# A new order of the engine pieces, and block 1 normalized with ScalarE's negated mean

## The chip, the cores and the metric

The kernel runs on one core of one Trainium2 chip. The core has a matrix engine (TensorE, "PE" in the profile, with its weight loads shown apart as "PEld"), VectorE ("DVE"), ScalarE ("ACT"), GpSimd ("POOL"), SyncE ("SP", here only a queue that issues DMAs) and sixteen DMA engines. Each engine works through its own list of instructions in the order in which they stand in the program and waits on semaphores for the others. The metric is the device time of one execution in microseconds (us); lower is better.

## What is computed

The input x has 2048 rows of 640 features. Each row is normalized (mean and variance over the 640 features), and the normalized xn feeds two branches whose results are added to x:

```python
x = A_x
xn = _layernorm(x, axis=-1)
return x + _A_ref(xn, A_wqkv, A_wo) + _B_ref(xn, B_w1, B_b1, B_w2, B_b2)
```

Branch A is attention with 32 heads of 20 features in which row s looks at eight rows only: s, s-2, ... s-14. It needs q, k, v (xn times a 640x1920 matrix), the eight logits of each row and head, a softmax over the eight, the weighted sum of v, and a product with a 640x640 matrix. Branch B is a two-layer perceptron: 640 to 1536, tanh-approximated gelu, 1536 back to 640, with biases b1 and b2.

## The kernel before

The 2048 rows are four chunks n = 0..3 of 512 rows, and a chunk is four blocks bl = 0..3 of 128 rows. Every piece of work has a short name and a function that emits its instructions; the list `ORDER` at the top of the file gives all the names in one sequence, and the last lines of the kernel emit them in that sequence. So `ORDER` alone sets the order of the instructions on every engine, on the DMA queue of SP and on that of POOL. Semaphore waits are put in by a tracker that looks at which buffers an instruction reads and writes.

What the names mean, with the engine:

- Statistics and normalization. `st` (VectorE) takes mean and variance of a block; for block 1 of chunk 0 and for chunks 2 and 3 ScalarE does it instead with a sum (`sum1`, `su`), a negated mean (`neg1`, `ng`) and a sum of squares (`sq1`, `sq`). `rs` (ScalarE, a logarithm and an exponential) gives 1/std. `rc` (VectorE) gives -mean/std for a chunk. `xn` writes the normalized block: chunk 0 on VectorE, chunks 1 to 3 on ScalarE. `mean1` (VectorE, one 128x1 instruction, L241) turns ScalarE's sum of block 1 into its mean.
- Transposes. Chunk 0 is transposed on TensorE (`tp`) and copied out (`tc`); chunks 1 to 3 by DMA from SP's queue (`tc`).
- q, k, v: for chunk 0 `ga`, `gb`, `gd`, `ge`, `hj` on TensorE, evicted from PSUM by ScalarE (`gc`, `hc`); for the others `pj{n}{which}{to}` on TensorE and `pc` on ScalarE. `pad` copies the last 14 columns of the previous chunk's k or v in front of this chunk's, so that the window of eight rows can reach back; `pad11` is that copy for k of chunk 1 (L409, ScalarE).
- Attention: `qk{n}{j}` (VectorE) multiplies q with eight shifted windows of k for block j; `pa` and `pb` (VectorE) add up features; `lg` (TensorE) sums over a head; `cp`, `mask`, `m`, `mx`, `ex`, `ss`, `ri`, `at` are the softmax on VectorE and ScalarE; `xe` spreads the weights by DMA from SP's queue; `av`, `ac`, `ad`, `ot` (VectorE, some `ac` by DMA from POOL's queue) are the weighted sum.
- Perceptron and output: `f1{n}_{ft}` (TensorE) and `ge` (ScalarE, gelu, which evicts PSUM); `t{n}{s}{pc}` (TensorE) computes the output of chunks 0 to 2 with rows and columns exchanged, `u` (ScalarE) evicts it, `ut` (SP's queue) transposes it by DMA, `ud` (POOL's queue) adds it into the output in HBM, where `xp{n}` (SP's queue) has put x before. Chunk 3 is computed straight (`o3{bl}{pc}`, `ohi`), added to x on VectorE (`dl`, `dh`) and written (`dd`, `dlo`, `dhi`).
- Loads from SP's queue: `ldx` (x of chunks 2 and 3), `ld2` (w2, four DMAs), `ldo` (the output matrix of branch A, three DMAs). `tb`, `b1` and `ho` are small set-up steps (a bias transpose on TensorE, its copy on VectorE, and a reduction on VectorE).

Buffers that tie the engines together: PSUM has four rotating one-bank buffers for `hj`, `pj`, `f1` and the like (pool `psA`), two for `t` (`psO`), and one two-bank tile for `lg` (`psL`). ScalarE has two sets of function tables, one for gelu and one for log and exp; going from one to the other emits a table load (L170).

Of the kernel before, what the change touches and what calls it, by code (L numbers as in the profile page):

```python
# [11 lines left out]
ALU = mybir.AluOpType  # L12
# [4 lines left out]
S, D, F, H, W, DIL = 2048, 640, 1536, 32, 8, 2  # L17
# [20 lines left out]
COLS = ((0, 2), (2, 4), (4, 5))  # L38

ORDER = """  # L40
pad01 pad02 st00a st00 sum1 rs00 neg1 xn00a sq1 xn00b tp00a wa tp00b tc00a wb ga tc00b rs01 mean1 gb2 xn01a gb3 xn01b
tp01a st03a tp01b gb4 tc01a tc01b st02a gd gc0 st02 ge st03 rs02 hj101 xn02 rs03 gc4 xn03 gc1 tp02 st13a tp03 st11a
hj100 tc03 st10a st10 tc02 hj102 st13 hc101 hj012 hc100 st12a hj112 st12 hc102 tb hj111 st11 b1 ho rs1 hj110 hc112 rc1
qk00 hc012 pk xn11 hj011 xn10 tc11 hj200 hc111 hc110 tc10 qk01 hj010 hc011 hc200 f10_11 xn13 hc010 tc13 f10_0 xn12
qk03 f10_3 tc12 f10_1 ge0_11 ldx ge0_0 qk02 f10_5 ge0_1 pj110 ge0_5 ld2 pj114 pc110 pa00 su20 pj102 ge0_3 pj100 pc102
pa01 su22 pj112 pc100 su21 f10_2 pb01 pc114 pj103 ge0_2 pc112 xp2 hj201 su23 pb04 ldo pj101 hc201 ng2 sq22 pj104 pad11
pc103 lg0 pj111 cp0b cp0a pc101 mask pj113 m0b xp0 pc104 m0a pc111 xp1 hj211 pc113 mx0a mx0b pj120 qk10 ex0a pj122
pc120 ex0b t040 sq21 qk11 pj124 pc122 hc211 hj210 sq23 t000 sq20 ss0b hj212 hc210 f10_7 ss0a ri0b pc124 pj121 qk13 rs2
hc212 ri0a f10_4 pc121 f10_6 rc2 qk12 f10_8 ge0_4 ge0_7 t001 xn21 f11_1 xn20 tc21 at0b ge0_8 pa11 t041 ge0_6 tc20
pj123 f11_10 xn23 pa10 ge1_1 tc23 f11_9 xn22 ge1_10 f10_9 tc22 at0a pc123 pb11 ge1_9 hj202 xe01 su33 t042 xe03 f11_3  # L50
pad21 xe00 su32 pb14 pj210 ge1_3 xe02 pj203 pc210 su31 lg1 hc202 t002 su30 av01 pj204 ng3 ge0_9 pj214 sq32 pc204 pj211
av00 pc203 ac01 pad12 pc214 pj200 sq30 f11_0 pc200 pc211 av02 ac00 f11_5 sq31 cp1a f10_10 cp1b ge1_0 pj213 av03 ge0_10
ge1_5 pj201 pc213 sq33 t003 pj221 m1 t043 mx1 rs3 pj224 pc221 ac03 ex1 pj202 pc201 rc3 ss1 xn31 pj220 pc202 tc31 ac02
f11_6 pc224 ri1 pj223 at1 ad01 xe11 pj222 pc223 xe12 xe13 pj212 ad00 pc222 xn32 f12_3 xe10 pc220 ot00 xn33 f11_2 ot01
tc32 av11 t004 t044 u00 tc33 t010 u04 av12 t011 ut00 xn30 t012 t030 tc30 t013 av13 t014 ud00 t031 u01 ac11 t032 t033
ac12 t020 t034 ge1_6 av10 ge2_3 t021 pc212 t022 f12_4 ac13 ac10 t023 ge2_4 t024 u03 ut01 xb ad11 f12_6 ot11 pj302 qk22
f11_8 pc302 ge1_2 f11_7 pj303 qk23 ge1_7 ge1_8 pj311 ge2_6 pc303 pj300 pa21 t140 pc300 pj310 f11_11 ad10 pj314 ge1_11
ot10 pc311 f11_4 pc310 qk20 pj301 ge1_4 pc314 pj313 u02 pc301 ut02 t130 qk21 pc313 f13_6 pad31 pad22 ut03 t141 ut04
ud01 pj304 pa20 pj312 ud02 t142 pc312 f12_9 pb21 pc304 ud03 ge3_6 f13_4 t143 pb24 f12_2 f13_1 ge2_2 ge2_9 lg2 f12_10
qk31 cp2a ge3_4 t131 cp2b t132 t133 t134 m2 qk30 f13_0 f13_2 ge3_0 ge2_10 t144 u13 mx2 ge3_2 pj321 qk32 u14 ge3_1  # L60
pj322 t100 pa30 t110 ex2 t101 f13_5 qk33 t102 ge3_5 f13_10 pad32 pc321 pc322 t103 t104 ss2 t111 pa31 ri2 f12_0 u10
f13_3 ut10 at2 f13_8 pb31 xe20 t120 xe22 ge3_8 t112 xe21 ge2_0 t113 ge3_3 pb34 f12_8 xe23 t114 lg3 u11 f12_11 cp3a
av20 ut11 ud10 cp3b f13_9 ge2_11 ge3_10 f13_7 ge2_8 m3 ge3_9 f12_5 ac20 ge3_7 mx3 t121 av21 f12_1 ex3 t122 o300 ss3
t123 ac21 ge2_1 f13_11 av23 t124 ri3 o301 u12 f12_7 at3 av22 pj323 xe31 ge2_5 ut12 ud11 ud04 ge2_7 pj324 t200 t201
ac22 xe30 t230 ut13 pj320 ac23 o302 pc320 ad21 pc323 t202 pc324 xe33 t231 ge3_11 ut14 ad20 t232 o310 ot21 t233 ot20
t203 o311 av31 t204 t234 u20 ut20 av30 t210 u23 ud12 t211 xe32 t212 t213 t214 ac30 t220 u21 ac31 t221 t222 t223 ad30
t224 av33 t240 u22 ud13 ud20 ut21 ud14 t241 t242 t243 ac33 o330 o331 t244 o303 u24 ud21 ut22 ot30 o320 av32 o304 ud22
ut23 ut24 o321 ud23 o312 ac32 o313 dh0 dl0 o332 ad31 o322 dd0 o314 ud24 ot31 o323 dl1 o324 dh1 dd1 o333 dl2 o334 dh2
dd2 ohi dl3 dlo dh3 dhi
""".split()  # L70


# [1 line left out]
def kernel(  # L74
# [16 lines left out]
    nc = tc.nc  # L91
# [75 lines left out]
    def table(name):  # L167
# [6 lines left out]
    mask = consts.tile([H, W, MW], BF16, name="mask")  # L174
    nc.gpsimd.memset(mask[:], 0.0)
    nc.gpsimd.affine_select(
        out=mask[:],
# [16 lines left out]
    mv = consts.tile([P, NCH * BPC, nc.vector.BN_AGGR_DIM], F32, name="mv")  # L194
# [3 lines left out]
    acc = consts.tile([P, NCH * BPC], F32, name="acc")  # L198
    neg = consts.tile([P, NCH * BPC], F32, name="neg")
# [17 lines left out]
    def xn_tile(n, bl):  # L217
        return get(("xn", n, bl), lambda: lnp.tile([P, D], BF16, tag="xn", name="xn"))

    def col(tile_, n, bl):  # L220
        i = n * BPC + bl
        return tile_[:, i : i + 1]
# [14 lines left out]
            accum_out=mv[:, n * BPC + bl, 1:2],  # L237
        )

    def do_mean1():  # L240
        nc.vector.tensor_scalar(  # L241
            out=mv[:, 1, 0:1], in0=col(acc, 0, 1), scalar1=1.0 / D, scalar2=None, op0=ALU.mult
        )

    def do_rs(n, b0, b1):
        sl = slice(n * BPC + b0, n * BPC + b1)
        summed = n in ACT_STATS or (n, b0) == (0, 1)
        table(LOG_SET)
        nc.scalar.activation(
            logv[:, sl], mv[:, sl, 1], ACT.Ln, bias=eps_t[:], scale=1.0 / D if summed else 1.0  # L250
        )
        nc.scalar.activation(rstd[:, sl], logv[:, sl], ACT.Exp, scale=-0.5)
# [10 lines left out]
    def do_xn(n, bl, a=0, b=KT):  # L263
        i, cs = n * BPC + bl, slice(a * P, b * P)
        xn = xn_tile(n, bl)
        if n:
            nc.scalar.activation(xn[:], x_sb[:, i, :], ACT.Identity, bias=col(nmr, n, bl), scale=col(rstd, n, bl))
            return
        nc.vector.tensor_scalar(
            out=xn[:, cs],  # L270
            in0=x_sb[:, i, cs],
            scalar1=mv[:, i, 0:1],
            scalar2=rstd[:, i : i + 1],
            op0=ALU.subtract,
            op1=ALU.mult,
        )

# [444 lines left out]
    def piece(name, fn, *args):  # L722
        assert name not in pieces
        pieces[name] = lambda: fn(*args)

    for name in "tb b1 mean1 ho ldx ld2 ldo ohi mask pk xb".split():
        piece(name, locals()[f"do_{name}"])
    for u, a, b, eng in (("a", 0, 2, "ve"), ("b", 2, KT, "se")):
        for bl in range(2):
            piece(f"xn0{bl}{u}", do_xn, 0, bl, a, b)  # L730
            piece(f"tp0{bl}{u}", do_tp, 0, bl, a, b, True)
        piece(f"tc00{u}", do_tc, 0, 0, a, b, "ve")
        piece(f"tc01{u}", do_tc, 0, 1, a, b, eng)
    for bl in range(BPC):
        if bl != 1:
            piece(f"st0{bl}a", do_st, 0, bl, 0)
            piece(f"st0{bl}", do_st, 0, bl, 1)
        piece(f"rs0{bl}", do_rs, 0, bl, bl + 1)
        if bl > 1:
            piece(f"xn0{bl}", do_xn, 0, bl)  # L740
            piece(f"tp0{bl}", do_tp, 0, bl, 0, KT)
            piece(f"tc0{bl}", do_tc, 0, bl, 0, KT, "se")
# [17 lines left out]
    for n in range(NCH):  # L760
        if n:
            piece(f"rs{n}", do_rs, n, 0, BPC)
            piece(f"rc{n}", do_rc, n, 0, BPC)
            if n in ACT_STATS:
                piece(f"ng{n}", do_ng, n, 0, BPC)
            for bl in range(BPC):
                if n in ACT_STATS:
                    piece(f"su{n}{bl}", do_su, n, bl)
                    piece(f"sq{n}{bl}", do_sq, n, bl)
                else:  # L770
                    piece(f"st{n}{bl}a", do_st, n, bl, 0)
                    piece(f"st{n}{bl}", do_st, n, bl, 1)
                piece(f"xn{n}{bl}", do_xn, n, bl)
                piece(f"tc{n}{bl}", do_td, n, bl)
            for which in range(3):
                for to in range(KT):
                    piece(f"pj{n}{which}{to}", do_pj, n, which, to)
                    piece(f"pc{n}{which}{to}", do_pc, n, which, to)
# [83 lines left out]
```

## Time and profile before

| | |
|---|---|
| Time, median of 3 runs | 206.21 us (205.78 to 206.46) |
| The profiled execution's own time | 205.85 us |
| Its span, first to last instruction | 203.8 us |
| PE busy | 199.1 us (98%), 1082 matmuls recorded |
| DVE busy | 186.3 us (91%), 161 instructions |
| ACT busy | 128.7 us (63%), 237 instructions |
| Granted TensorE clock | 1.000 over the whole span |
| DMA | 27.31 MB moved, mean 134 GB/s |

Times in the views are counted from the start of the span. The page gives the share of each engine, the chain of work that ended last, and groups of equal instructions with their mean duration and the idle time before them; the timeline gives single instructions in order of time, where a row with "x2" merges two neighbours and idle time before a row stands in brackets with what ended it.

### The profile page before, as it was taken

How to read it: one execution, taken by the hardware profiler on the slowest of the kernel's cores; microseconds unless marked ns; L12 is line 12 of the kernel's file. 1: busy time of each engine (PE TensorE's matmuls, PEld its weight loads, DVE VectorE, ACT ScalarE, POOL GpSimd, SP SyncE). 2: the span in 40 equal slices, each digit the busy share in tenths (PEclk: the TensorE clock that was granted, in tenths of full speed). 3: DMA queues.
4: the chain of work that ended last, by engine and by line, in shares of the span. 5: the costliest groups of instructions: out<-in, count | busy, mean ns of one | idle time of the engine just before them, and what ended most of it. 6: DMA issues, size and time to landing. Idle time of an engine off the chain costs nothing.

```text
span 203.8 us, 2855 instructions
## 1 busy us (share of the span) xinstructions
PE 199.1 (98%) x1082; PEld 105.7 (52%) x1100; DVE 186.3 (91%) x161; ACT 128.7 (63%) x237; POOL 29.4 (14%) x34
## 2 busy tenths in 40 slices
PE   8999999999999999999999999999999999999994
PEld 3999456564454455444454443444434454444552
DVE  2899999699998999999999997999978999998972
ACT  5679988799899997647264635398669923221000
POOL 2000000000000400004420040000202704046210
PEclk9999999999999999999999999999999999999999
DMA  6996499910246681779896190000496799897851
GB/s 213 388 397 197 120 328 341 400 72 3 64 86 184 112 148 32 164 147 117 144 152 71 37 92 0 3 0 0 92 186 123 126 169 129 97 106 88 77 90 64
DMA packets 38430, 27.31 MB, mean 134 GB/s; under 512 B 25106, under 2 KB 34578, under 8 KB 38418
## 3 DMA queue, kind: packets, MB, share of 16 engines
q1 hardware_dynamic: 28016, 20.39, 37.4%
q0 software_dynamic: 10080, 6.56, 27.2%
q10 hardware_dynamic: 322, 0.20, 0.3%
q8 instruction: 8, 0.13, 0.3%
q14 instruction: 4, 0.03, 0.0%
HBM read 10.49 MB, written 4.59 MB: 74 GB/s over the span
## 4 chain that ended last, share of the span: by engine, by line
PE 96%; ACT 1%; issue 1%; DVE 0%
PE T L701 27%; PE hps L619 25%; PE pps L338 23%; PE gps L382 7%; PE lo L657 5%; PE idle L448 2%; PE both L657 2%; PE gps L351 2%; PE hi L657 1%; PE L L485 1%; ACT x_sb L704 1%; PE tp L284 1%; ACT wq_sb L635 1%; ACT hT L635 0%; DVE prod L669 0%
## 5 line engine op out<-in xcount | busy, mean ns | idle before, releaser
L619 PE MATMUL hps<-xnT,w_sb 128*128 128x512 bf16 x231 | 55.8, 379 | 0.4
L435 DVE TENSOR_TENSOR prod<-qT,kT 128x5120 bf16<-128x5120 bf16 x16 | 44.6, 2820 | 1.2 <-PE L L485 1.0
L701 PE MATMUL T<-hT,w_sb 128*128 128x512 bf16 x179 | 44.0, 379 | 0.1
L619 PEld LDWEIGHTS <-w_sb 128*128 128x128 bf16 x240 | 23.3, 98 | 28.0 <-issue 1.0
L713 POOL DMA_DIRECT2D out_dram<-x_sb x15 | 19.7, 1430 | 84.0 <-DMA x_sb<-x_sb 63.0
L635 ACT ACTIVATE hT<-hps,bT 128x512 bf16<-128x512 f32 x36 | 23.5, 686 | 9.4 <-PE hps L619 9.1
L701 PEld LDWEIGHTS <-w_sb 128*128 128x128 bf16 x180 | 17.4, 98 | 20.5 <-issue 0.4
L704 ACT ACTIVATE x_sb<-T,bT 128x512 bf16<-128x512 f32 x15 | 10.3, 687 | 21.8 <-PE T L701 14.8
L589 DVE TENSOR_TENSOR prod<-vT,ax 128x5120 bf16<-128x5120 bf16 x8 | 22.3, 2821 | 1.8 <-PE L L485 1.8
L589 DVE TENSOR_TENSOR prod<-vT,x_sb 128x5120 bf16<-128x5120 bf16 x8 | 22.3, 2820 | 0.1
L600 POOL DMA_DIRECT2D prod<-prod x6 | 7.8, 1300 | 80.4 <-DVE prod L589 80.4
L170 ACT ACT_TABLE_LOAD x14 | 18.0, 1283 | 1.0 <-PEq L846 0.7
L476 DVE TENSOR_TENSOR prod<-prod 128x4096 bf16<-128x4096 bf16 x8 | 18.3, 2290 | 0.2
L338 PE MATMUL pps<-xnT,wq_sb 128*128 128x512 bf16 x74 | 18.3, 379 | 0.1
L701 PE MATMUL T<-oT,wo 128*128 128x512 bf16 x73 | 18.2, 379 | 0.1
L470 DVE TENSOR_TENSOR prod<-prod 128x4096 bf16<-128x4096 bf16 x8 | 18.1, 2286 | 0.1
L338 PE MATMUL pps<-xnT,wk_sb 128*128 128x512 bf16 x75 | 18.2, 379 | 0.0
L338 PE MATMUL pps<-xnT,wv_sb 128*128 128x512 bf16 x71 | 17.8, 379 | 0.2
L602 DVE TENSOR_TENSOR prod<-prod 128x2560 bf16<-128x2560 bf16 x10 | 14.7, 1488 | 0.1
L338 PEld LDWEIGHTS <-wk_sb 128*128 128x128 bf16 x75 | 8.7, 118 | 7.7 <-issue 0.4
L338 PEld LDWEIGHTS <-wv_sb 128*128 128x128 bf16 x75 | 8.8, 117 | 7.4
L338 PEld LDWEIGHTS <-wq_sb 128*128 128x128 bf16 x75 | 8.8, 117 | 7.3
(96 smaller groups left out, 241.5 us busy)
## 6 DMA issues: line engine op xcount, KB each, us to landing
prod<-prod POOLq DMA_DIRECT2D x6, 640.0 KB, 7.0
ax<-attn SPq DMA_DIRECT2D x8, 256.0 KB, 4.3
x_sb<-attn SPq DMA_DIRECT2D x8, 256.0 KB, 4.8
w_sb<-in_B_w_dram SPq DMA_DIRECT2D x2, 960.0 KB, 11.3
w_sb<-in_B_w_dram SPq DMA_DIRECT2D x4, 480.0 KB, 8.2
out_dram<-x_sb SPq DMA_DIRECT2D x3, 640.0 KB, 9.5
out_dram<-x_sb POOLq DMA_DIRECT2D x15, 128.0 KB, 5.1
x_sb<-in_A_x_dram SPq DMA_DIRECT2D x2, 640.0 KB, 6.9
```

The lines of the kernel that those rows point to most:

```text
L170: nc.scalar.preload_act_table_set(name)
L338: nc.tensor.matmul(ps[:], lhsT=wqkv_p[which][:, ti, to, :], rhs=xnT[:, ti, :], start=(ti == 0), stop=(ti == KT - 1),)
L435: nc.vector.tensor_tensor(out=prod[:, j], in0=q[:, :, at].unsqueeze(1).to_broadcast([P, W, KT, P]), in1=window(k, at), op=ALU.mult,)
L470: nc.vector.tensor_tensor(out=low, in0=low, in1=high, op=ALU.add)
L476: nc.vector.tensor_tensor(out=first, in0=first, in1=rows[:, :, t * P : (t + 1) * P], op=ALU.add)
L589: nc.vector.tensor_tensor(out=prod[:, j], in0=window(qkv_tile(n, 2), slice(j * P, (j + 1) * P)), in1=ax_view(n)[:, j, :, :].unsqueeze(2).t ...
L602: nc.vector.tensor_tensor(out=low, in0=low, in1=high, op=ALU.add)
L619: nc.tensor.matmul(ps[:], lhsT=w1_sb[:, ti, ft * P : (ft + 1) * P], rhs=tiles["xnT", n][:, ti, :], start=(ti == 0), stop=(ti == KT - 1),)
L635: nc.scalar.activation(hT, tiles["hps", n, ft][:], ACT.Gelu_apprx_tanh, bias=bT[:, ft : ft + 1], scale=1.0)
L657: nc.tensor.matmul(out_ps(bl, hi), lhsT=lhs, rhs=rhs[:, CH:D] if hi else rhs[:, 0:CH], start=pc == 0 and k == 0, stop=pc == 4 and k == len ...
L701: nc.tensor.matmul(ps[:], lhsT=lhs, rhs=rhs, start=pc == 0 and k == 0, stop=pc == 4 and k == len(srcs) - 1)
L713: nc.gpsimd.dma_start(dst, src, accum_op=ALU.add)
```

## The change

Two things change. The names in `ORDER` stand in another sequence, on nearly every line. And `mean1` is gone: the two normalizing instructions of block 1 add ScalarE's negated mean (`neg`, column 1, written by `neg1`) where they subtracted the mean that `mean1` had made. The number of matmuls, of evictions and of table loads (14) is the same, and so is every other instruction.

The diff, cut to the code and to those lines of `ORDER` that the text speaks of:

```diff
 ORDER = """
-pad01 pad02 st00a st00 sum1 rs00 neg1 xn00a sq1 xn00b tp00a wa tp00b tc00a wb ga tc00b rs01 mean1 gb2 xn01a gb3 xn01b
-tp01a st03a tp01b gb4 tc01a tc01b st02a gd gc0 st02 ge st03 rs02 hj101 xn02 rs03 gc4 xn03 gc1 tp02 st13a tp03 st11a
...
-qk03 f10_3 tc12 f10_1 ge0_11 ldx ge0_0 qk02 f10_5 ge0_1 pj110 ge0_5 ld2 pj114 pc110 pa00 su20 pj102 ge0_3 pj100 pc102
-pa01 su22 pj112 pc100 su21 f10_2 pb01 pc114 pj103 ge0_2 pc112 xp2 hj201 su23 pb04 ldo pj101 hc201 ng2 sq22 pj104 pad11
-pc103 lg0 pj111 cp0b cp0a pc101 mask pj113 m0b xp0 pc104 m0a pc111 xp1 hj211 pc113 mx0a mx0b pj120 qk10 ex0a pj122
-pc120 ex0b t040 sq21 qk11 pj124 pc122 hc211 hj210 sq23 t000 sq20 ss0b hj212 hc210 f10_7 ss0a ri0b pc124 pj121 qk13 rs2
-hc212 ri0a f10_4 pc121 f10_6 rc2 qk12 f10_8 ge0_4 ge0_7 t001 xn21 f11_1 xn20 tc21 at0b ge0_8 pa11 t041 ge0_6 tc20
...
-ac22 xe30 t230 ut13 pj320 ac23 o302 pc320 ad21 pc323 t202 pc324 xe33 t231 ge3_11 ut14 ad20 t232 o310 ot21 t233 ot20
...
-ut23 ut24 o321 ud23 o312 ac32 o313 dh0 dl0 o332 ad31 o322 dd0 o314 ud24 ot31 o323 dl1 o324 dh1 dd1 o333 dl2 o334 dh2
-dd2 ohi dl3 dlo dh3 dhi
+pad01 pad02 st00a st00 sum1 ho rs00 neg1 xn00a sq1 xn00b tp00a wa tp00b wb tc00a tc00b rs01 ga xn01a gb2 xn01b tp01a
+gb3 st02a tb tp01b tc01a gb4 st02 tc01b gd gc0 st03a ge rs02 st03 hj101 b1 xn02 rs03 gc4 xn03 gc1 tp02 st12a tp03
...
+qk02 f10_1 tc12 ge0_0 f10_5 ldx qk03 f10_11 ge0_5 f10_3 ge0_11 ge0_2 pj101 ge0_3 pa00 pj112 pc101 ge0_1 pj104 pc112
+xp2 pa01 su20 pj110 xp0 pc104 ld2 su22 pj102 pc110 pb01 pj100 su21 hj201 su23 pc102 pb04 pj103 ng2 pc100 hc201 pj114
+sq22 lg0 pc114 ldo pj111 cp0b cp0a sq21 mask pj113 m0b pc103 m0a pj124 pc111 mx0a pc113 mx0b t000 qk11 pj120 ex0b
+hj202 ex0a hj210 pc120 sq23 ss0a hj211 pc124 ss0b sq20 pj122 qk13 hc202 rs2 f10_7 pad11 hc211 pc122 t040 ri0b f10_8
+ri0a rc2 qk12 hc210 f10_4 f11_1 ge0_7 xn21 qk10 f11_3 ge0_4 tc21 xn20 pj121 ge1_3 tc20 t041 ge1_1 pa11 f11_9 ge0_8
...
+t002 xe00 ge0_9 pj123 pad21 su32 pb14 pj210 xe02 su31 pj203 xp1 pc210 su30 lg1 t042 pc203 av01 cp1b f10_10 ng3 f11_5
...
+o320 pc320 o321 at3 ac22 o302 xe31 ut13 pj324 ad20 f12_11 pc324 ad21 t232 xe30 ge2_11 xe32 t202 ut14 ot21 f13_11 ot20
+t203 av31 t204 t233 u20 t234 ut20 av30 t210 u23 ud12 xe33 t211 t212 t213 t214 ac30 t220 u21 ac31 t221 ge3_11 t222 av33
...
+o330 ut24 ac32 o322 ud23 o313 ac33 o304 ad31 o331 ud24 o323 dl0 dh0 o314 ot31 dd0 o324 dl1 dh1 dd1 o332 dl2 o333 dh2
+dd2 o334 ohi dl3 dlo dh3 dhi
 """.split()
...
-    def do_mean1():
-        nc.vector.tensor_scalar(
-            out=mv[:, 1, 0:1], in0=col(acc, 0, 1), scalar1=1.0 / D, scalar2=None, op0=ALU.mult
-        )
...
         nc.vector.tensor_scalar(
             out=xn[:, cs],
             in0=x_sb[:, i, cs],
-            scalar1=mv[:, i, 0:1],
+            scalar1=neg[:, 1:2] if bl == 1 else mv[:, i, 0:1],
             scalar2=rstd[:, i : i + 1],
-            op0=ALU.subtract,
+            op0=ALU.add if bl == 1 else ALU.subtract,
             op1=ALU.mult,
         )
...
-    for name in "tb b1 mean1 ho ldx ld2 ldo ohi mask pk xb".split():
+    for name in "tb b1 ho ldx ld2 ldo ohi mask pk xb".split():
         piece(name, locals()[f"do_{name}"])
```

## The prediction

> **What bounds the kernel now.** I read the page first: shares, chain and groups.
>
> ```profile
> PE 199.1 (98%) x1082; PEld 105.7 (52%) x1100; DVE 186.3 (91%) x161; ACT 128.7 (63%) x237; POOL 29.4 (14%) x34
> ...
> PE 96%; ACT 1%; issue 1%; DVE 0%
> ...
> L619 PE MATMUL hps<-xnT,w_sb 128*128 128x512 bf16 x231 | 55.8, 379 | 0.4
> ...
> L170 ACT ACT_TABLE_LOAD x14 | 18.0, 1283 | 1.0 <-PEq L846 0.7
> ```
>
> TensorE carries 96% of the chain, and its big groups have almost no idle time before them: 0.4 us in 55.8 for L619. The other engines are hidden behind it as long as it never waits. Next I read the chain in order of time, where the rate shows.
>
> ```profile
> 35.88 0.55 PE L L485 x8
> 36.42 2.29 PE pps L338 x10
> 38.71 1.09 PE gps L382 x10
> ...
> 41.96 0.65 PE T L701 x3
> 42.61 1.08 PE pps L338 x5
> ```
>
> Five 512-column matmuls take 1.08 us (0.216 each), ten 256-column ones 1.09. These rates hold from 6 us to 200.86 us, broken only by gaps of 0.05 us. The change keeps every matmul, so it can hardly gain: what it can do is make TensorE wait. The question is which wait, so I then read the timelines of ScalarE, which frees TensorE's PSUM buffers, and VectorE, around the place where `pad11` goes.
>
> ```profile
> 35.31 0.23 ACT L409 COPY kT<-kT 128x70 bf16<-128x70 bf16 x1
> ...
> 37.20 0.58 ACT L525 CAST e<-L 128x512 bf16<-128x512 f32 x1 [1.18 <-DVE e L525]
> 37.68 1.08 ACT L402 CAST qT<-pps 128x512 bf16<-128x512 f32 x2
> ...
> 47.98 0.35 ACT L397 CAST vT<-gps 128x256 bf16<-128x256 f32 x1
> 48.24 0.26 ACT L557 ACTIVATE ax<-ax 128x64 f32<-128x64 f32 x1
> 48.53 0.26 ACT L558 ACTIVATE rs<-ax 128x64 bf16<-128x64 f32 x1
> 48.69 0.57 ACT L402 CAST vT<-pps 128x512 bf16<-128x512 f32 x1
> 49.27 1.28 ACT L170 ACT_TABLE_LOAD   x1
> 50.57 1.26 ACT L635 ACTIVATE hT<-hps,bT 128x512 bf16<-128x512 f32 x2
> 51.72 1.73 ACT L267 ACTIVATE xn<-x_sb,nmr,rstd 128x640 bf16<-128x640 bf16 x2
> ```
>
> L409 is `pad11`: at 35.31 us it waits for nothing. From 37.20 to about 54.6 us ScalarE has no idle gap worth a bracket: over the span it is busy 63%, here it is full. VectorE beside it:
>
> ```profile
> 40.12 5.56 DVE L435 TENSOR_TENSOR prod<-qT,kT 128x5120 bf16<-128x5120 bf16 x2
> 45.59 0.42 DVE L532 TENSOR_TENSOR ax<-e 128x256 f32<-128x256 bf16 x1
> ...
> 47.44 2.82 DVE L435 TENSOR_TENSOR prod<-qT,kT 128x5120 bf16<-128x5120 bf16 x1
> ```
>
> A `qk` takes 2.82 us (2.74 to the next start) and the two folds of the softmax sum 1.85 (45.59 to 47.44).
>
> **The change, part by part.** *`pad11`, the part that decides.* Its place moves behind `qk11`, `qk13` and `rs2`. It writes the k tile of chunk 1 that those products read, and in the changed program it waits for VectorE's count to reach the one that `qk13` sets. ScalarE works in order, so everything behind it waits too: evictions `hc211`, `pc122` and `hc210`, the softmax's `ri0b`, `ri0a`, a table load, and the gelus `ge0_7`, `ge0_4` that free TensorE's buffers.
>
> When does `qk13` end? VectorE: `qk11` at 40.12, the folds now between, then `qk13`: 40.12 + 2.74 + 1.85 + 2.82 = 47.53.
>
> When is ScalarE there? From 37.20: copy 0.48, three squares 2.6, three q/k evictions 1.44, table load 1.30, two exponentials 1.06, two v evictions 0.94, `hc202` 0.26, `rs2` 0.44: 8.5 us, so at 45.7. It stands idle 1.8 us with work waiting.
>
> When is `ge0_4` done? From 47.55: `pad11` 0.14, two evictions 0.96, two log/exp pairs 0.90, `hc210` 0.58, table load 1.30, `ge0_7` 0.58, `xn21` 0.81, `ge0_4` 0.69: 5.96 us, so at 53.5.
>
> When does TensorE want that buffer? The work up to `lg0` is the same, so `lg0` again ends at 36.42. Up to `pj121` come ten groups of five at 1.08, two output pieces at 0.65 and 25 matmuls of 256 columns at 0.109: 14.8 us, plus two 0.05 us gaps: 51.3. At that point the four buffers hold `f10_8`, `f10_4`, `f11_1`, `f11_3`, and `pj121` takes the one that `ge0_4` frees. TensorE waits in steps, already before `f10_8`, 53.5 - 51.3 = 2.2 us in all. Bounds: 1.6, if each row of ScalarE is 0.05 us shorter; 2.7, if VectorE's softmax steps run 0.5 us later because one more square stands before the last k eviction. I take 2.2, the value of the rows themselves. After it ScalarE is ahead again: `ge1_3`, wanted next, is done at 53.5 + 0.7 + 0.6 + 0.1 = 54.9, and TensorE asks at 55.3 (53.5 plus 1.08 and 0.65). VectorE is late with nothing: `lg1` moves from 62.7 to about 64.9, its last `pb` is done near 63.
>
> One price inside that sum is disputed. The table load is 1283 ns in the group row, and the next gelu starts 0.02 us after it, so I use 1.30. The Trainium skill (ScalarE: Activation LUTs, What ACT_TABLE_LOAD costs) adds a drain of about 1380 ns to every switch of sets, 2.66 us in all. By that the wait would be about 3.6 us and the time 209.8; the trace's next row, at 0.02 us, disagrees.
>
> *`mean1` and the head.* The instruction takes 0.14 us on VectorE (6.48), behind a copy and just before the normalization of block 1 at 6.71. TensorE does twenty matmuls from 6.38 to 7.71 before it needs that block, which is ready at 7.35, so the cover is 0.3 us. `tp01a` now stands five matmuls (0.33 us) earlier, and the block comes 0.1 earlier: cover about 0.1, cost nothing. Bounds -0.14 (all on the path) to +0.2 (cover gone). `ho` (0.28) falls into VectorE's 0.66 us wait before 4.93; `b1` (0.12) into the wait for `rs02`. `tb` goes from 13.98 to about 7.5 and needs the two small bias loads, issued by 2.28 us: the nearest load took 2.6 us and the slowest of that time 9.5, so 0 to +4; I take 0, since these 4 KB stand directly behind x of block 1, which landed at 3.52.
>
> *First gelus and projections.* Six `f1` pieces instead of five stand before the first `pj`, so the DMA transposes (last one landed 24.20) have 1 us more. Cost 0.
>
> *SP's queue.* `xp2` and `xp0` go ahead of the four w2 loads and `ldo`. `xp2` waits for x of chunk 2, which before was there at 27.82 at the latest. Then 0.86 and 0.62 us of issue: w2 from 29.3 instead of 24.72. The first w2 load took 6.7 us to land, the last 9.7: ready at 36.0 to 39.0. `t000` reads it at 36.42 + 3.24 = 39.7 (before 41.96). Cost 0; with the 11.3 us of the w1 loads it would be +0.9, but then ahead of the 2.2 and mostly inside it, since `qk13` does not wait for that. `xp1` goes behind the first `xe`, 15 us before `xe1` needs it: 0.
>
> *The last chunk.* `xe33` now stands in SP's queue behind `ut20`, which waits for a TensorE piece. Before, the weights used last had landed at 179.99 and were used at 188.52. By the rows `xe33` is issued about 2 us behind `ut20` and lands 3.6 to 5.1 us later, 0 to 1.1 us after VectorE could use it. VectorE has 1.5 us to wait anyway at `ot30`, for TensorE to be done with oT. So 0, bound +1. At the very end `o324` comes 0.65 us (three matmuls) sooner behind `ot31`, which had 0.7 us to spare: 0, bound +0.4.
>
> Sum: 205.85 (the profiled execution's own time, 0.36 under the median) + 2.2 = 208.05; against the median 206.21 + 2.2 = 208.4.
>
> **The rivals.** *The wait is absorbed.* Place: `pad11`. If it waited for `qk11` alone (42.9) or for nothing, ScalarE would pass it at 45.7, end `ge0_4` at 51.7 and cost 0.35 us: 206.6. It decides by whether `pad11` can start before about 45.9. For it: its 14 columns are not those that block 3 reads. Against it: the wait in the program, and no gap in ScalarE's rows here to take it.
>
> *TensorE has room.* If its 98% only looked full, 2 us would vanish in it: 206.2. Against it: 0.216 us per 512 columns from end to end, with no faster stretch. The Trainium skill (Trainium Kernel Development and Optimization, Performance Expectations) calls matmul busy time a bad measure and wants the weight loads' share. By that rule the 52% of PEld would mean headroom; the steady 1.08 us of the chain speaks against it.
>
> *More than one wait.* The bounds above come true: bias loads, w2, `xe33` or `ot31`. One or two of them add 0.6 to 1.4: 209.0 to 209.8. For it: covers of 0.1 to 0.7 us. Against it: they lie in different stages with their own slack.
>
> **How the numbers follow.** Within 0.3% is 0.6 us, about what a measurement of this kernel can tell. The forecast (+1.6 to +2.7, time 208.4) gets 0.66; more than one wait 0.16; absorbed 0.10; room in TensorE 0.05; a gain from the head, at most 0.14 us plus the loss of stalls that I do not see, 0.03. Slower 0.82, same 0.14, faster 0.04. The range reaches from 206.9 (206.21 + 0.7: two thirds of the wait absorbed) to 209.8, the upper end of the third rival. The forecast's own range is 207.8 to 208.9.
>
> **What would show it.** In the profile of the changed kernel: the pad copy on ScalarE near 47.5 us with about 1.8 us idle before it, ended by a VectorE `qk`; TensorE's idle time between 46 and 54 us adding up to about 2 us, ended by ScalarE's gelu or an eviction; the same rate of 1.08 us before and after; `lg1` near 65. No idle time in front of the transposes of block 1, of `t000`, of the last chunk's second product. Wrong, if the pad copy starts by 46 us, if TensorE shows its waits elsewhere, or if the time is within 0.6 us of 206.2.

## The result and the profile after

| | before | after |
|---|---|---|
| Time, median | 206.00 us (205.78 to 206.46, 6 runs) | 207.81 us (207.52 to 208.22, 6 runs) |
| The profiled execution's own time | 205.85 us | 207.52 us |
| Its span | 203.8 us | 205.4 us |
| Granted TensorE clock | 1.000 | 1.000 |

The ratio of the times is 1.0086, with a 95% interval of 1.007 to 1.0102: 1.81 us slower, where 2.2 us were forecast.

The lines of the page of the changed kernel that answer to those shown of before (busy time, the chain's shares by engine, two groups):

```profile
PE 200.2 (97%) x1100; PEld 105.1 (51%) x1100; DVE 185.7 (90%) x160; ACT 129.0 (63%) x237; POOL 29.4 (14%) x34
...
PE 90%; DVE 5%; ACT 3%; issue 0%
...
L614 PE MATMUL hps<-xnT,w_sb 128*128 128x512 bf16 x240 | 56.3, 379 | 1.5 <-ACT vT L392 1.0
...
L170 ACT ACT_TABLE_LOAD x14 | 18.0, 1283 | 1.0 <-PEq L841 0.7
```

The shares hardly differ. The chain does: TensorE had 96% of it and now has 90%; the rest went to VectorE and ScalarE. The group L614 (L619 before) had 0.4 us of idle time before its matmuls and now has 1.5, most of it ended by an eviction on ScalarE. In order of time, the chain of the changed kernel leaves TensorE at 36.20 us, when `lg0` is done, and runs through VectorE's softmax and `qk11`. The next view shows the rest of this stretch (start, duration, engine, tile, line) up to the return to TensorE:

```profile
42.67 0.35 DVE ax L527
...
44.51 2.75 DVE prod L430
47.28 0.25 ACT kT L404
47.53 0.49 ACT vT L392
...
49.88 1.28 ACT L170
51.17 0.69 ACT hT L630
51.86 0.81 ACT xn L262
52.67 0.59 ACT hT L630
...
53.30 1.24 PE pps L333 x5
```

This is the path of the forecast, link by link: `qk13` on VectorE, `pad11` (L404), the evictions and the table load queued behind it, `ge0_7`, `xn21`, `ge0_4`, and then `pj121`. The timeline of ScalarE in the same execution (in brackets: idle time before, and what ended it):

```profile
45.32 0.21 ACT L247 ACTIVATE rstd<-logv 128x4 f32<-128x4 f32 x1
47.28 0.25 ACT L404 COPY kT<-kT 128x70 bf16<-128x70 bf16 x1 [1.75 <-DVE prod L430]
```

ScalarE was done with `rs2` at 45.53 and stood idle for 1.75 us until `qk13` ended. TensorE's timeline shows what that cost:

```profile
46.22 0.81 PE L696 MATMUL T<-hT,w_sb 128*128 128x512 bf16 x3
48.07 3.40 PE L614 MATMUL hps<-xnT,w_sb 128*128 128x512 bf16 x15 [1.03 <-ACT vT L392]
51.91 1.24 PE L614 MATMUL hps<-xnT,w_sb 128*128 128x512 bf16 x5 [0.44 <-ACT hT L630]
53.30 1.24 PE L333 MATMUL pps<-xnT,wv_sb 128*128 128x512 bf16 x5
```

The brackets count idle time from the modelled end of a matmul. From start to start, with 0.216 us for a matmul, the three waits are 1.20, 0.61 and 0.31 us: 2.12 us in all. After 9 us there is one other wait of TensorE over 0.12 us in this trace: 0.21 us at 44.07, behind the last 256-column matmul. In the kernel before, the same stretch has no bracket:

```profile
45.81 1.24 PE L619 MATMUL hps<-xnT,w_sb 128*128 128x512 bf16 x5
46.89 1.24 PE L338 MATMUL pps<-xnT,wv_sb 128*128 128x512 bf16 x5
47.97 3.40 PE L619 MATMUL hps<-xnT,w_sb 128*128 128x512 bf16 x14
51.21 0.81 PE L701 MATMUL T<-hT,w_sb 128*128 128x512 bf16 x3
51.85 1.24 PE L619 MATMUL hps<-xnT,w_sb 128*128 128x512 bf16 x5
```

To compare executions I cut the span at two marks: the start of `lg0`, and the start of the last matmul. In microseconds:

| Kernel | `lg0` starts | `lg0` to `lg1` | `lg0` to last matmul | last matmul to end |
|---|---|---|---|---|
| before | 35.81 | 26.91 | 164.82 | 3.20 |
| after | 35.53 | 28.97 | 166.88 | 2.98 |

The middle grew by 2.06 us, all of it between `lg0` and `lg1`. The head is 0.28 us shorter and the tail 0.22 us shorter in this pair of executions. Together that is the 1.6 us by which the spans differ.

### The profile page after: what moved, and what is told of

It reads as the page before. It is cut to its first block, busy times and chain, and to the rows that moved or that the text cites. A ratio compares the mean times of both kernels' runs of the same rounds, so it can differ in the third digit from the quotient of the medians.

```text
span 205.4 us, 2870 instructions
## 1 busy us (share of the span) xinstructions
PE 200.2 (97%) x1100; PEld 105.1 (51%) x1100; DVE 185.7 (90%) x160; ACT 129.0 (63%) x237; POOL 29.4 (14%) x34
## 4 chain that ended last, share of the span: by engine, by line
PE 90%; DVE 5%; ACT 3%; issue 0%
PE T L696 26%; PE hps L614 23%; PE pps L333 21%; PE lo L652 5%; PE gps L377 5%; DVE prod L430 3%; PE idle L443 2%; PE both L652 2%; PE gps L346 1%; PE hi L652 1%; PE L L480 1%; DVE ax L529 1%; PE tp L279 1%; ACT L170 1%; ACT hT L630 1%; DVE ax L527 1%
## 5 line engine op out<-in xcount | busy, mean ns | idle before, releaser
L614 PE MATMUL hps<-xnT,w_sb 128*128 128x512 bf16 x240 | 56.3, 379 | 1.5 <-ACT vT L392 1.0
L696 PE MATMUL T<-hT,w_sb 128*128 128x512 bf16 x180 | 44.6, 379 | 0.0
L614 PEld LDWEIGHTS <-w_sb 128*128 128x128 bf16 x240 | 23.4, 98 | 29.8 <-issue 2.3
L708 POOL DMA_DIRECT2D out_dram<-x_sb x15 | 20.8, 1593 | 67.1 <-DMA x_sb<-x_sb 67.1
L595 POOL DMA_DIRECT2D prod<-prod x6 | 7.3, 1208 | 100.2 <-DVE prod L584 100.2
L333 PE MATMUL pps<-xnT,wv_sb 128*128 128x512 bf16 x75 | 18.3, 379 | 0.2
L397 ACT CAST qT<-pps 128x512 bf16<-128x512 f32 x15 | 8.6, 583 | 7.2 <-PE pps L333 7.2
```

Source lines behind the costliest of these rows:

```text
L333: nc.tensor.matmul(ps[:], lhsT=wqkv_p[which][:, ti, to, :], rhs=xnT[:, ti, :], start=(ti == 0), stop=(ti == KT - 1),)
L614: nc.tensor.matmul(ps[:], lhsT=w1_sb[:, ti, ft * P : (ft + 1) * P], rhs=tiles["xnT", n][:, ti, :], start=(ti == 0), stop=(ti == KT - 1),)
L696: nc.tensor.matmul(ps[:], lhsT=lhs, rhs=rhs, start=pc == 0 and k == 0, stop=pc == 4 and k == len(srcs) - 1)
L708: nc.gpsimd.dma_start(dst, src, accum_op=ALU.add)
```

## The experiments

Theory A is that of the prediction: the pad copy waits for `qk13` and holds ScalarE's in-order queue, so TensorE runs out of PSUM buffers. Theory B: something else in the new order costs the time. Theory C: it is the lateness of the pad columns themselves. These are the readings of all runs, each against the kernel before on the same chip:

| Run | median, us | ratio to before (95%) | `lg0` starts | `lg0` to `lg1` | `lg0` to last matmul |
|---|---|---|---|---|---|
| e1_pad_early | 205.87 | 0.9976 (0.9957 to 0.9995) | 36.41 | 26.95 | 164.86 |
| e2_pad_mid | 206.12 | 0.9988 (0.9967 to 1.0009) | 36.78 | 27.09 | 165.00 |
| e3_turned | 207.44 | 1.0048 (1.0023 to 1.0072) | 35.69 | 28.18 | 166.09 |
| e4_pool | 206.34 | 0.9998 (0.9972 to 1.0025) | 35.74 | 27.35 | 165.26 |
| e5_before_pad_late | 208.34 | 1.0117 (1.0104 to 1.013) | 36.00 | 29.29 | 167.21 |
| e6_before_no_mean1 | 205.85 | 0.9995 (0.9986 to 1.0003) | 35.81 | 26.91 | 164.82 |
| e7_pad_early_mean1 | 205.90 | 1.0003 (0.9992 to 1.0015) | 35.93 | 27.05 | 164.96 |
| e8_dose | 211.35 | 1.0268 (1.0246 to 1.029) | 35.92 | 32.48 | 170.39 |
| e9_half_dose | 210.12 | 1.0219 (1.0191 to 1.0246) | 35.67 | 30.37 | 168.28 |
| e10_pad_early_again | 205.76 | 0.9989 (0.9977 to 1.0) | 35.72 | 27.08 | 164.99 |
| e11_changed_again | 207.79 | 1.0091 (1.0074 to 1.0109) | 35.90 | 28.97 | 166.88 |

The first four shared one chip, the others a second one in two sittings (four and three), each with its own runs of before. On the first chip the times scatter more: before had a median of 206.50 us there (205.72 to 209.14), and 205.95 and 205.94 on the second. So the columns from one profile say more about the first four than their medians do.

**The pad copy early again.** One name moves in the changed order:

```diff
-sq22 lg0 pc114 ldo pj111 cp0b cp0a sq21 mask pj113 m0b pc103 m0a pj124 pc111 mx0a pc113 mx0b t000 qk11 pj120 ex0b
-hj202 ex0a hj210 pc120 sq23 ss0a hj211 pc124 ss0b sq20 pj122 qk13 hc202 rs2 f10_7 pad11 hc211 pc122 t040 ri0b f10_8
+sq22 pad11 lg0 pc114 ldo pj111 cp0b cp0a sq21 mask pj113 m0b pc103 m0a pj124 pc111 mx0a pc113 mx0b t000 qk11 pj120 ex0b
+hj202 ex0a hj210 pc120 sq23 ss0a hj211 pc124 ss0b sq20 pj122 qk13 hc202 rs2 f10_7 hc211 pc122 t040 ri0b f10_8
```

> The changed kernel with one piece moved: pad11 stands ahead of lg0, as in the kernel before. Everything else keeps the changed order. Theory A (the pad copy waits for the product qk13, holds ScalarE's in-order queue and starves TensorE of PSUM buffers): no idle time of ScalarE ended by VectorE near 47 us, TensorE's three waits between 46 and 54 us (2.11 us) gone, lg1 near 62.4 instead of 64.5, and the time 207.8 - 2.1 = 205.7, at most 206.0. Theory B (the rest of the new order costs it: SP's queue, VectorE's order, the last chunk): the waits stay somewhere and the time stays at 207.8.

> The first experiment's kernel (pad11 ahead of lg0) once more, beside the changed kernel on the same chip. Theory A: 2.0 us below the changed kernel; against the kernel before 0.0 to -0.3 us, since everything else of the change lies behind TensorE.

> The changed kernel itself once more, so that the comparison with pad11 early is made on one chip: 207.8, TensorE's three waits between 46 and 54 us again 2.1 us in all, whatever the moment at which TensorE comes to its full rate (5.77 us in the first profile of it, 4.3 to 6.7 in the others).

The medians were 205.87 and 205.76 us. In the third sitting, where both ran, the changed kernel took 207.79: 2.03 us more for the place of one copy. TensorE's timeline in the second profile with the copy early, over the stretch that held the waits:

```profile
46.41 0.81 PE L696 MATMUL T<-hT,w_sb 128*128 128x512 bf16 x3
47.06 4.48 PE L614 MATMUL hps<-xnT,w_sb 128*128 128x512 bf16 x20
51.47 1.24 PE L333 MATMUL pps<-xnT,wv_sb 128*128 128x512 bf16 x5
```

The same twenty matmuls now run without a break. `lg1` started at 63.35 and 62.80 us rather than the 62.4 expected, because `lg0` was later too; from `lg0` to `lg1` it is the time of before. Theory B falls: all the rest of the new order is still there, and costs nothing in this stage. Against the kernel before, the version is 0 to 0.5 us faster by the second run's interval (0.1 to 0.9 by the first, on the chip that scatters), too little to call it a gain.

**The pad copy late, but ahead of the product.** In the changed order `pad11` moves behind `sq23`:

```diff
-hj202 ex0a hj210 pc120 sq23 ss0a hj211 pc124 ss0b sq20 pj122 qk13 hc202 rs2 f10_7 pad11 hc211 pc122 t040 ri0b f10_8
+hj202 ex0a hj210 pc120 sq23 pad11 ss0a hj211 pc124 ss0b sq20 pj122 qk13 hc202 rs2 f10_7 hc211 pc122 t040 ri0b f10_8
```

> The changed kernel with pad11 placed behind sq23, which is behind qk11 but still ahead of ss0a and of qk13. It is 8 us later on ScalarE than in the kernel before, and chunk 1's first columns of k are later by as much. Theory A: ScalarE reaches it near 43.4 us, qk11 ended at 42.6, so it waits for nothing; time 205.7 to 206.0. Theory C (it is the lateness of the pad columns for VectorE's next product that costs, whatever the pad copy waits for): qk12 is not later here either, so 205.7 to 206.0 too. Theory B: 207.8.

It came to 206.12 us. The copy ran at 44.68 us with no wait before it. The 1.3 us over the 43.4 of the expectation are the later head of this execution (`lg0` at 36.78). TensorE lost 0.15 us once, on an eviction of v (0.46 us to the next start where 0.31 is usual). A late copy as such costs next to nothing; a copy behind `qk13` costs 2 us.

**The wait turned round.** Only `qk13` moves, behind `pad11`:

```diff
-hj202 ex0a hj210 pc120 sq23 ss0a hj211 pc124 ss0b sq20 pj122 qk13 hc202 rs2 f10_7 pad11 hc211 pc122 t040 ri0b f10_8
+hj202 ex0a hj210 pc120 sq23 ss0a hj211 pc124 ss0b sq20 pj122 hc202 rs2 f10_7 pad11 qk13 hc211 pc122 t040 ri0b f10_8
```

> The changed kernel with qk13 moved behind pad11 in the written order; each engine's own sequence stays the same, only the direction of the wait between the two turns round. ScalarE then passes the pad copy at 45.5 us instead of 47.28, and VectorE may have to wait for the pad copy before qk13 (it would start at 45.7 instead of 44.4). Theory A: no idle time on ScalarE there and no waits of TensorE between 46 and 54 us (2.1 us gained). If VectorE is made to wait, its chain to the second chunk's sums is 1.3 us later, the last pb ends near 63.8 where TensorE wants lg1 at 62.4: up to 1.4 us come back there, time 207.1; if VectorE is not tied, 205.7. Theory B: 207.8 with the waits where they were.

The median was 207.44 us. From the timelines of ScalarE, VectorE and TensorE in its profile:

```profile
45.58 0.23 ACT L404 COPY kT<-kT 128x70 bf16<-128x70 bf16 x1
...
45.85 2.83 DVE L430 TENSOR_TENSOR prod<-qT,kT 128x5120 bf16<-128x5120 bf16 x1 [1.18 <-ACT kT L404]
...
63.87 0.62 PE L480 MATMUL L<-prod,head_of 128*32 128x512 bf16 x8 [1.02 <-DVE prod L471]
```

ScalarE no longer waits, and TensorE's waits behind it are gone but for 0.24 us at 51.1. VectorE waits instead, 1.18 us, and hands it on 18 us later: `lg1` stands still for 1.18 us from start to start (1.395 less a matmul's 0.216). From `lg0` to the last matmul the kernel is 1.23 us behind the first experiment, where up to 1.4 was expected if VectorE is tied; the medians differ by 1.57 us (207.44 against 205.87). So the pair is tied in both directions, although the columns are disjoint: the copy writes columns 0 to 13 of each strip of 526, and block 3 with its window reads columns 384 to 525. Only `qk10`, which stands later, reads the first 14.

**The copy on another engine.** The pad copy keeps its late place and moves to GpSimd:

```diff
-            nc.scalar.copy(dest[:, :, 0:PAD], pair_of(1, 1)[:, :, 2 * P :])
+            nc.gpsimd.tensor_copy(dest[:, :, 0:PAD], pair_of(1, 1)[:, :, 2 * P :])
```

> The changed kernel with the pad copy in its new place but issued on GpSimd instead of ScalarE. GpSimd has nothing queued there, so the wait for qk13 (47.3 us) remains and holds nobody's queue. Theory A: no idle time on ScalarE near 47 us, no waits of TensorE between 46 and 54 us. GpSimd's copy is slower than ScalarE's 0.25 us, so qk12 starts 0.4 to 1.0 us later and lg1 may wait 0 to 1.2 us for it: 205.7 to 206.9. Theory C (the late pad columns themselves): 207.8 or more. Theory B: 207.8 with TensorE's waits where they were.

It took 206.34 us. From the timelines of GpSimd, VectorE and TensorE in its profile:

```profile
47.59 0.24 POOL L404 COPY kT<-kT 128x70 bf16<-128x70 bf16 x1 [45.53 <-ACT rs L553]
...
47.87 5.56 DVE L430 TENSOR_TENSOR prod<-qT,kT 128x5120 bf16<-128x5120 bf16 x2 [0.35 <-POOL kT L404]
...
63.09 0.61 PE L480 MATMUL L<-prod,head_of 128*32 128x512 bf16 x8 [0.19 <-DVE prod L471]
```

The copy starts right after `qk13`, so it is as late as in the changed kernel, and nobody stands behind it. (The bracket names ScalarE, but the copy's start, 0.14 us behind the end of `qk13` at 47.45, shows what it waited for.) Two microseconds become 0.4 (165.26 against 164.86 from `lg0` to the last matmul): VectorE starts `qk12` 0.35 us late, and `lg1` has to wait for that. Theory C falls: what costs is the queue behind the copy. GpSimd's copy took 0.24 us here, about as long as ScalarE's 0.25; I had expected it to be slower.

**The wait put into the kernel before.** Two products change places in the order of before, and the copy goes between them:

```diff
-pa01 su22 pj112 pc100 su21 f10_2 pb01 pc114 pj103 ge0_2 pc112 xp2 hj201 su23 pb04 ldo pj101 hc201 ng2 sq22 pj104 pad11
-pc103 lg0 pj111 cp0b cp0a pc101 mask pj113 m0b xp0 pc104 m0a pc111 xp1 hj211 pc113 mx0a mx0b pj120 qk10 ex0a pj122
-pc120 ex0b t040 sq21 qk11 pj124 pc122 hc211 hj210 sq23 t000 sq20 ss0b hj212 hc210 f10_7 ss0a ri0b pc124 pj121 qk13 rs2
+pa01 su22 pj112 pc100 su21 f10_2 pb01 pc114 pj103 ge0_2 pc112 xp2 hj201 su23 pb04 ldo pj101 hc201 ng2 sq22 pj104
+pc103 lg0 pj111 cp0b cp0a pc101 mask pj113 m0b xp0 pc104 m0a pc111 xp1 hj211 pc113 mx0a mx0b pj120 qk13 ex0a pj122
+pc120 ex0b t040 sq21 qk11 pad11 pj124 pc122 hc211 hj210 sq23 t000 sq20 ss0b hj212 hc210 f10_7 ss0a ri0b pc124 pj121 qk10 rs2
```

> The kernel before with the wait put into it: qk10 and qk13 change places and pad11 stands right behind qk11, so that ScalarE meets it early. Nothing else of the new order. Theory A (a ScalarE copy that waits for VectorE is enough): ScalarE reaches the pad copy near 43.4 us, where VectorE's qk11 ends between 45.5 and 45.7; it stands idle about 2.2 us and TensorE, with four PSUM buffers to fill, loses 1.5 to 2.2 us behind it: 207.5 to 208.2. Theory B (the rest of the new order costs the time): 206.0, no wait of TensorE.

The median was 208.34 us, 0.1 above the range. From the timelines of ScalarE and TensorE:

```profile
45.95 0.25 ACT L409 COPY kT<-kT 128x70 bf16<-128x70 bf16 x1 [2.27 <-DVE prod L435]
...
46.74 0.70 PE L382 MATMUL gps<-xnT,wv_sb 128*128 128x256 bf16 x5 [1.12 <-ACT vT L402]
49.47 1.24 PE L338 MATMUL pps<-xnT,wv_sb 128*128 128x512 bf16 x5 [0.94 <-ACT vT L397]
```

ScalarE waits 2.27 us; TensorE loses 1.29 and 1.11 us from start to start, 2.40 in all, and from `lg0` to the last matmul the kernel is 2.39 us behind before. With nothing else of the new order, the one wait makes the loss.

**The second part of the change alone, and undone.** In the kernel before, `mean1` is taken out and `xn` of block 1 uses the negated mean, as the change does it; and in the first experiment's kernel `mean1` is put back (the diff is that of the second of these, without the function itself):

```diff
-pad01 pad02 st00a st00 sum1 ho rs00 neg1 xn00a sq1 xn00b tp00a wa tp00b wb tc00a tc00b rs01 ga xn01a gb2 xn01b tp01a
+pad01 pad02 st00a st00 sum1 ho rs00 neg1 xn00a sq1 xn00b tp00a wa tp00b wb tc00a tc00b rs01 ga mean1 xn01a gb2 xn01b tp01a
...
-            scalar1=neg[:, 1:2] if bl == 1 else mv[:, i, 0:1],
+            scalar1=mv[:, i, 0:1],
...
-            op0=ALU.add if bl == 1 else ALU.subtract,
+            op0=ALU.subtract,
```

> The kernel before with only the second part of the change: mean1 is taken out and block 1 is normalized with ScalarE's negated mean. Prediction's step (the instruction is hidden behind TensorE's first matmuls): the same time as before within 0.15 us. If mean1 was on the path, 0.14 to 0.3 us less, and the first matmul of k (9.60 us before, 9.30 after the change) starts earlier by as much at the same moment of TensorE's full rate.

> The first experiment's kernel (pad11 ahead of lg0) with mean1 put back ahead of block 1's normalization. Prediction's step: within 0.15 us of the first experiment's time, 205.9. If mean1 was on the path of the head: 0.14 to 0.3 us more than that.

205.85 us against 205.95 of before (ratio 0.9995, interval 0.9986 to 1.0003), and 205.90 with `mean1` back against 205.87 and 205.76 without it. From `lg0` on, before without `mean1` has the very times of before. Whatever the instruction costs is not over 0.3 us, and probably nearer 0.1.

**A longer wait.** In the changed kernel `qk12`, whole or half, moves ahead of the pad copy. The other engines keep their order, and VectorE does only the small `rc2` behind `qk12` rather than ahead of it:

```diff
-hj202 ex0a hj210 pc120 sq23 ss0a hj211 pc124 ss0b sq20 pj122 qk13 hc202 rs2 f10_7 pad11 hc211 pc122 t040 ri0b f10_8
-ri0a rc2 qk12 hc210 f10_4 f11_1 ge0_7 xn21 qk10 f11_3 ge0_4 tc21 xn20 pj121 ge1_3 tc20 t041 ge1_1 pa11 f11_9 ge0_8
+hj202 ex0a hj210 pc120 sq23 ss0a hj211 pc124 ss0b sq20 pj122 qk13 qk12 hc202 rs2 f10_7 pad11 hc211 pc122 t040 ri0b f10_8
+ri0a rc2 hc210 f10_4 f11_1 ge0_7 xn21 qk10 f11_3 ge0_4 tc21 xn20 pj121 ge1_3 tc20 t041 ge1_1 pa11 f11_9 ge0_8
```

For the half, `do_qk` takes a range of the eight shifted windows, and the piece for windows 0 to 3 (`qh12`) takes the place that `qk12` has here; `qk12` keeps its old place with windows 4 to 7.

> The changed kernel with one more product ahead of the pad copy: qk12 moves in front of rc2 and of pad11. ScalarE's, TensorE's and SP's sequences stay as they are; VectorE only does the tiny rc2 behind qk12 instead of ahead of it. The pad copy now waits for qk12, 2.8 us longer: it starts near 50.05 us instead of 47.28. Theory A: each us of that wait reaches TensorE, whose waits between 46 and 56 us grow from 2.1 to about 4.9 us; lg1 near 67.3; 207.8 + 2.8 = 210.6. If the starved stretch has spare time left or the wait is not the cause: between 207.8 and 209.

> As the run with qk12 ahead of the pad copy, but with half of that product: qk12 is cut in two instructions of four shifted windows each, and only the first half (about 1.4 us) stands ahead of rc2 and pad11. The pad copy then starts near 48.7 us, 1.4 us later than in the changed kernel. With the full product TensorE lost 3.5 us more than in the changed kernel for 2.8 us more of wait, and its granted clock dropped after one idle stretch of 3.9 us. Theory A alone: TensorE's waits grow from 2.1 to 3.4 or 3.5 us, clock 1.000 throughout, 207.8 + 1.4 = 209.2. If the clock drops at this shorter stretch too: mean clock near 0.992, 209.5 to 210.

The timelines of ScalarE and TensorE with the half product:

```profile
48.82 0.25 ACT L404 COPY kT<-kT 128x70 bf16<-128x70 bf16 x1 [3.15 <-DVE prod L430]
...
49.61 3.40 PE L614 MATMUL hps<-xnT,w_sb 128*128 128x512 bf16 x15 [2.44 <-ACT vT L392]
53.45 1.24 PE L614 MATMUL hps<-xnT,w_sb 128*128 128x512 bf16 x5 [0.44 <-ACT hT L630]
```

In this execution, 209.3 us with a clock of 1.000, the three waits of TensorE are 2.60, 0.61 and 0.31 us from start to start: 3.52 in all, 1.40 more than in the changed kernel for 1.40 more on ScalarE (3.15 against 1.75). That is theory A to the hundredth. But the median was 210.12: of six executions two had a mean clock of 1.000 (209.3 and 209.83 us) and four had 0.991 or 0.992 (209.9 to 211.42 us). With the whole product all five executions had a clock of 0.984 to 0.992, and took 211.35 us. Its timelines of ScalarE and TensorE:

```profile
50.40 0.25 ACT L404 COPY kT<-kT 128x70 bf16<-128x70 bf16 x1 [4.49 <-DVE prod L430]
...
51.19 6.16 PE L614 MATMUL hps<-xnT,w_sb 128*128 128x512 bf16 x20 [3.77 <-ACT vT L392]
57.19 1.03 PE L333 MATMUL pps<-xnT,wv_sb 128*128 128x512 bf16 x4
```

And the same stretch cut into windows (window and its length, then busy time of TensorE, of its weight loads, VectorE, ScalarE and GpSimd, each with its count, then the granted clock and the DMA share and rate):

```profile
46.80:51.20 4.40, 0.63 (x4) 0.21 (x3) 4.16 (x4) 0.80 (x3) 0.00 (x0) 1.00 0.00 0
51.20:53.40 2.20, 2.20 (x8) 0.87 (x8) 2.20 (x1) 2.12 (x7) 0.00 (x0) 0.76 0.00 0
53.40:56.00 2.60, 2.60 (x8) 1.00 (x7) 2.60 (x3) 2.59 (x4) 0.00 (x0) 0.55 0.00 0
56.00:60.00 4.00, 4.00 (x21) 1.88 (x19) 4.00 (x4) 3.21 (x6) 0.00 (x0) 1.00 0.58 86
```

Twenty matmuls took 6.16 us where they take 4.48 when undisturbed. After 3.94 us of idleness (4.15 less 0.216) TensorE resumed at 51.19 at its full rate, and from 52.6 to 55.9 us gave 0.426 us per matmul instead of 0.216. The slower clock made the matmuls 1.68 us longer, and in that time ScalarE caught up: no second and third wait appears, which were 0.92 us in the changed kernel. 3.94 + 1.68 = 5.62 us, against 5.57 by the marks (170.39 - 164.82). Theory A alone gives 2.12 + 2.74 = 4.86 us, as ScalarE waited 2.74 us longer (4.49 against 1.75). The drop of the clock cost about 0.8 us in the end, and so say the medians (211.35 - 207.79 - 2.74 = 0.82). So the slope of one held from 1.75 to 3.15 us of wait on ScalarE as long as the clock stayed at 1.000, and broke upwards with the drop.

## Why the prediction was right

*`pad11`.* Right in place, path and size. ScalarE's idle time was to be 1.8 us and was 1.75; the copy was to run at 47.5 and ran at 47.28, with this execution 0.28 us ahead. `ge0_4` was to be done 17.7 us after the start of `lg0` (53.5 - 35.81) and was, at 53.25 - 35.53 = 17.72. The term that was a little off is TensorE's own way to `pj121`. My sum had it 15.5 us after the start of `lg0` (51.3 - 35.81). With the copy early and no wait it was 15.75 (51.47 - 35.72): I had allowed two gaps of 0.05 us, where TensorE stops for 0.20 us behind the last 256-column matmul (0.314 to the next start instead of 0.109) and for 0.10 us ahead of `pj121`. So the wait was 2.06 by the marks and 2.12 by the starts, where I wrote 2.2. In the kernel before, too, the gaps were not all of 0.05 us, as I had read: from start to start TensorE lost 0.19 us at 58.08 and some 0.1 us ahead of `lg1`.

*Where the other 0.2 us lies.* The time rose by 1.81 us, and by 1.85 in the later sitting, with 2.03 of it undone by the copy's place. The rest of the change is thus worth about -0.2 us (-0.5 to 0.0, from the ratio 0.9989 with its interval). My steps put it at 0 with bounds of both signs. From `lg0` to the last matmul the rest costs or gains under 0.2 us (164.86 and 164.99 against 164.82), so it should lie ahead of `lg0` or behind the last matmul. Those two stretches vary from execution to execution by more than that: the tail from 2.98 to 3.35 us, `lg0` from 35.53 to 36.78. `mean1` may be part of it, with 0.1 us (-0.3 to +0.1). More than this the runs do not settle.

*The head.* TensorE's first matmul of k started at 9.30 us after the change and at 9.60 before, and it would have been easy to credit `mean1`. It is another thing. The matmuls of 128 columns start every 0.107 us at first and every 0.056 us later; the step came at 6.7 us in the profile of before, at 5.8 in that of after. Over all thirteen profiles it lies between 3.7 and 6.7, with no regard to the kernel: at 4.0 in before without `mean1`, at 5.1 in the second profile of the changed kernel, at 6.6 in the half dose. The Trainium skill (TensorE: Matmul & The Clock Gate, What's actually happening) says that the clock opens by an activity window of 3413 ns that runs freely and doesn't start with the kernel, so that the moment differs from run to run. The traces agree, and the spread, 3.0 us, is within such a window. The profile's record of the clock begins only at this step, so the granted clock of 1.000 in the tables leaves out the slow matmuls ahead of it. An earlier step need not make the head shorter: in before without `mean1` the first matmul of k started at 9.23, 0.37 us earlier than in before, but TensorE then waited 0.41 us from start to start at 23.84 for the first gelu, and `lg0` started at 35.81 in both.

*The steps at nothing.* SP's queue: w2 was issued from 28.40 (29.3 in the forecast), and `t000` ran at 39.35 without a wait, as forecast. `tb` ran at 7.43 without one. Among the first `f1` pieces TensorE waited 0.11 us at 23.56, where I had put none. The last chunk: from `lg3` to the last matmul 51.13 us before and 51.14 after, so `xe33` and `ot31` cost nothing.

*The rivals.* The absorbed wait would have given 206.6: its condition, a copy that can start by 45.9, was not met, though the third experiment shows that nothing in the data demanded the wait. That TensorE has room is refuted by every dose: its waits of 2.12, 2.40 and 3.52 us came out as 2.06, 2.39 and 3.46 from `lg0` to the last matmul (166.88, 167.21 and 168.28 less 164.82), with the weight loads' share at 51%. So the weight loads' share, one of the two measures that the Trainium skill gives (Trainium Kernel Development and Optimization, Performance Expectations), misleads here if it is read alone; the other, the arithmetic done as a share of the peak (MFU), was left out of the prediction and not worked out. More than one wait did not come. And the price of a switch of tables that the Trainium skill gives (ScalarE: Activation LUTs, What ACT_TABLE_LOAD costs) would have needed 209.8: the load at 49.88 took 1.28 us and the gelu behind it began at 51.17, 1.29 us after the load's start.

## What to carry to other kernels

The price of a cheap copy in an in-order queue is not its 0.25 us but its wait, paid by all that is queued behind it. When a piece is moved past an instruction that touches the same buffer, look up which way the tracker now ties the two, even where the columns are disjoint, and sum both engines' rows up to that point: here 1.75 us of waiting came out as 2.1 us on TensorE. If the order can't be changed, put such a copy on an engine with nothing behind it (0.4 us instead of 2.0), and compare traces by a stage that starts behind the noisy head.

## What the runs showed that I had not expected

A wait of TensorE can cost more than its own length. Idle stretches up to 1.3 us left the mean granted clock at 0.999 or 1.000 (the changed kernel and the wait put into before). With the half product, whose profile shows a stretch of 2.6 us, the mean fell to 0.991 or 0.992 in four of six executions; with the whole one, 3.9 us, to between 0.984 and 0.992 in five of five. On the same chip none of the 83 executions of the other kernels fell. On the chip of the first four runs 5 of 83 did, three of them of the kernel before, which has no such wait; so a long wait isn't the only thing that goes with a drop, and what went with those five is open.

The one drop that was profiled can be cut exactly at the moments at which the clock changed. These windows of the full and, last, of the half dose are all 3.41 us long (columns as above):

```profile
48.94:52.35 3.41, 1.16 (x6) 0.57 (x6) 3.17 (x3) 1.88 (x7) 0.00 (x0) 1.00 0.00 0
52.35:55.76 3.41, 3.41 (x10) 1.22 (x9) 3.41 (x3) 3.38 (x6) 0.00 (x0) 0.50 0.00 0
55.76:59.17 3.41, 3.41 (x18) 1.60 (x16) 3.41 (x4) 3.19 (x6) 0.00 (x0) 1.00 0.64 92
...
47.56:50.97 3.41, 1.36 (x7) 0.65 (x7) 3.17 (x4) 2.08 (x8) 0.00 (x0) 1.00 0.00 0
```

The clock was halved for 3.41 us, from 52.35 to 55.76, beginning 1.2 us after TensorE had resumed. One such stretch in 209.3 us makes a mean of 0.992, two make 0.984, so the means of the other executions that fell fit one drop or two. The Trainium skill (TensorE: Matmul & The Clock Gate, What's actually happening) lets the clock fall after an idle window of about 3.4 us. A stretch of 2.6 us can hold no such window, and in the profiled drop the last 1.2 us ahead of it were full of work; so a window with little work seems to be enough. By the clock record of the profiles the full clock lasted 47.79 us ahead of the drop and 153.60 us behind it, and 197.97 or 201.39 us in the twelve profiles without a drop: 14, 45, 58 and 59 times 3.413 us. So the changes fall on a grid of windows, which starts between 3.7 and 6.7 us in the thirteen profiles and isn't set by the kernel. If the clock goes by the window just ended, TensorE was busy in 34% of it where the clock dropped (1.16 of 3.41 us), and in 40% of the last row, of the half dose, where it did not (1.36 of 3.41). That would make the same wait trip one execution and not the next, by where it lies in the windows. It rests on two profiles and isn't shown; of the four executions with the half product that fell there is no profile.
